# Keys and queries turned ahead of the values in a recurrent forward loop, and DMA issues moved between two queues in its backward loop

## The chip, the cores and the metric

The kernel runs on one core of a Trainium2 chip. TensorE (PE) multiplies matrices, VectorE (DVE), ScalarE (ACT) and GpSimd (POOL) work on tiles, and SyncE (SP) only issues DMA transfers; ScalarE and GpSimd issue some too, each from its own sequencer and in the order of its own instructions. The metric is the device time of one execution in microseconds, the median of several runs.

## The reference, cut to what matters

The program is a layer with a segmented recurrence, and its gradient for x, the first memory and seven weights.

```
xn = layernorm(x)                               # 2048 tokens of 640
mem = mem0                                      # 8 rows of 640
for s in range(64):                             # segments of 32 tokens
    h = concat([mem, xs])                       # 40 rows
    q, k, v = h @ Wq, h @ Wk, h @ Wv            # 32 heads of 128
    p = softmax(where(mask, q @ k.T * scale, -1e9))
    o = (p @ v) @ Wo
    mem, out_s = o[:8], o[8:]                   # the 8 rows go to the next segment
out = x + concat(out_s) * silu(FFN(xn))         # FFN: w1, w3, w2 with silu
grads = vjp(out)(grad_out)
```

The eight memory rows make both passes a chain of 64 steps: forward from segment 0 to 63, backward from 63 to 0.

## The kernel before, in words

Each engine's instructions stand in the order in which the program writes them (`in_order`), so the written text is the schedule. Two loops of 64 steps are touched.

**Forward** (`recurrence`). `chain(t, gap)` writes the chain of step t: it projects the memory rows, with 24 token rows that ride along, onto keys, queries and values, turns keys and queries so that heads lie on partitions (`packed_sel`), scores the eight memory queries, normalises, multiplies by values and by `Wo`, and folds the result into the next step's input `hx`. Between its parts it calls `gap("W0")`, `gap("W1")` and so on to `gap("G6")`. `FILL` puts independent work into these gaps: up to three pieces a step, here called units, each of four heads and the token rows of three segments. A unit goes through `ld` (rows are loaded), `turn_q`, `scores`, `soft_max`, `soft_exp`, `norm`, `turn_p` and `pv`. Steps come in threes, with 3, 3 and 2 units. `WARM` is a table of dummy products of TensorE (line 940) at the end of a gap.

`stage()` gives one of two staging buffers of 128x1024: in a step the keys take one (`sk`), the queries the other (`sq`), the values the first again (`sv`). So ScalarE's first copy into `sv` must follow the store of the keys (`dump(sk, k.KS...)`, line 635, issued by SyncE). Three banks of PSUM, `bA`, `bB` and `bC`, serve the whole chain by turns; five others (tag "x") serve the units.

**Backward** (`phase4_Abwd`). Here too `chain(t, gap)` is the chain and `gap_of` the filling. A unit is loaded by `ld` (four transfers: memory rows `QVM`, token rows of queries and values, token rows of the gradient, and probabilities `PR`), into one of four buffers, and goes through `turn`, `dprob`, `dsoft` and `gmem`; `gmem_ld` runs `gmem` and loads the next unit into the buffer that this frees. The chain loads its own state for the step to come: `loads` (values, probabilities, queries; SyncE), `load_k` (keys, four transfers) and `load_xp` (one). After three products with `WvT`, `WkT` and `WqT` the chain folds the sum of two halves: ScalarE copies one half (`fup`, line 351), VectorE adds (`gfsz`, line 355), TensorE turns it (line 370), and the next step begins.

SyncE's and ScalarE's transfers report on the same small set of completion semaphores, given out in the order of the program; a transfer whose semaphore is still in use waits for the earlier one to land.

## Time and profile before

| | us |
|---|---|
| median of 3 runs | 4686.83 (4672.63 to 4691.8) |
| the profiled execution | 4689.95 |
| its span, first to last instruction | 4688.2 |
| forward loop, 62 steps from 398.0 to 1548.5 | 1150.5 |
| backward loop, 62 steps from 1820.0 to 2885.9 | 1065.9 |

| engine | busy us | share of the span |
|---|---|---|
| TensorE | 4342.0 | 93% |
| VectorE | 2235.9 | 48% |
| GpSimd | 2110.7 | 45% |
| ScalarE | 1604.0 | 34% |

The profile gives each instruction's engine, line, tiles, start and length, and the idle time of its engine just before with what seems to have ended it. A `q` behind an engine's name (ACTq, SPq) is its sequencer, which issues DMAs; while ScalarE's sequencer issues, ScalarE computes nothing new. The clock is the share of TensorE's full clock that was granted: 1.00 or, in some windows of 3.4 us, 0.5.

### The profile page before, as it was taken

How to read it: one execution, taken by the hardware profiler on the slowest of the kernel's cores; microseconds unless marked ns; L12 is line 12 of the kernel's file. 1: busy time of each engine (PE TensorE's matmuls, PEld its weight loads, DVE VectorE, ACT ScalarE, POOL GpSimd, SP SyncE). 2: the span in 40 equal slices, each digit the busy share in tenths (PEclk: the TensorE clock that was granted, in tenths of full speed). 3: DMA queues.
4: the chain of work that ended last, by engine and by line, in shares of the span. 5: the costliest groups of instructions: out<-in, count | busy, mean ns of one | idle time of the engine just before them, and what ended most of it. 6: DMA issues, size and time to landing. Idle time of an engine off the chain costs nothing.

```text
span 4688.2 us, 155303 instructions
## 1 busy us (share of the span) xinstructions
PE 4342.0 (93%) x62272; PEld 2843.6 (61%) x62272; DVE 2235.9 (48%) x7158; ACT 1604.0 (34%) x4487; POOL 2110.7 (45%) x3531
## 2 busy tenths in 40 slices
PE   8998989999999887999989998999999999999999
PEld 4544656566666545666666665676667666666675
DVE  8734666666666434555555553343224332311460
ACT  5532555555554423333333332232223322200000
POOL 6542555555555324455444444454335543311440
PEclk9998999999999998999999998999999999999999
DMA  7773666666665777787777775654445543579783
GB/s 265 240 253 110 182 182 182 180 180 185 181 178 170 172 175 217 205 227 202 222 207 205 200 214 143 148 162 132 111 115 158 144 128 106 173 214 216 157 181 100
DMA packets 976826, 834.49 MB, mean 178 GB/s; under 512 B 518890, under 2 KB 858286, under 8 KB 974144
## 3 DMA queue, kind: packets, MB, share of 16 engines
q1 hardware_dynamic: 667943, 509.49, 39.6%
q0 software_dynamic: 129952, 228.13, 16.6%
q10 hardware_dynamic: 178211, 86.95, 7.5%
q8 instruction: 492, 8.06, 0.8%
q14 instruction: 228, 1.87, 0.1%
HBM read 472.66 MB, written 310.33 MB: 167 GB/s over the span
## 4 chain that ended last, share of the span: by engine, by line
PE 45%; DMA 11%; issue 4%; DVE 2%; ACT 2%; SPq 1%; ACTq 1%; POOL 1%; POOLq 0%; DVEq 0%
PE wg L1692 11%; PE g L1673 9%; PE bank L339 5%; PE oa L1839 4%; PE wa L2227 2%; PE r6p L1623 2%; PE t6g L1655 2%; DMA DSR<-kTT 1%; PE pgxb L2160 1%; PE bank L320 1%; PE bank L1259 1%; DMA kTT<-VTD 1%; DMA kTT<-GOS 1%; PE bank L552 1%; PE t L1613 1%
## 5 line engine op out<-in xcount | busy, mean ns | idle before, releaser
L1692 PE MATMUL wg<-gr,hr 128*128 128x512 bf16 x2400 | 521.7, 379 | 0.0
L1673 PE MATMUL g<-land,ghacc 128*128 128x320 bf16 x3072 | 459.2, 300 | 0.8
L320 PEld LDWEIGHTS <-hx 128*32 128x32 bf16 x10240 | 285.6, 98 | 267.2 <-issue 37.2
L1692 PEld LDWEIGHTS <-hr 128*128 128x128 bf16 x2400 | 233.9, 98 | 278.9
L1673 PEld LDWEIGHTS <-ghacc 128*128 128x128 bf16 x3072 | 288.8, 98 | 103.6 <-ACT ghacc L92 2.2
L903 POOL DMA_DIRECT2D OR<-xv x163 | 99.1, 608 | 398.8 <-ACT xv L92 334.7
L90 DVE CAST wgo<-wg 128x512 bf16<-128x512 f32 x72 | 49.8, 692 | 471.2 <-PE wg L1692 471.2
L339 PEld LDWEIGHTS <-gkv 128*8 128x8 bf16 x8192 | 194.0, 89 | 89.5 <-issue 3.6
L90 DVE CAST stg<-bank 128x512 bf16<-128x512 f32 x256 | 177.0, 692 | 136.9 <-PE bank L320 125.8
L1349 POOL DMA_DIRECT2D VTD<-gvT x176 | 129.7, 741 | 248.4 <-ACT gvT L1348 233.0
L92 ACT COPY ghacc<-t6g 128x768 bf16<-128x768 bf16 (+1 forms) x176 | 137.2, 780 | 295.2 <-PE t6g L1655 282.2
L1638 POOL DMA_DIRECT2D GSP<-grs x48 | 25.6, 542 | 457.4 <-ACT grs L1630 456.8
L1679 DVE TENSOR_TENSOR ghacc<-ghacc,g 128x320 f32<-128x320 f32 x192 | 93.7, 488 | 209.7 <-PE g L1673 209.7
L92 ACT CAST wgo<-wg 128x512 bf16<-128x512 f32 x48 | 28.1, 586 | 479.8 <-PE wg L1692 406.9
L92 ACT CAST stg<-bank 128x512 bf16<-128x512 f32 x128 | 75.3, 589 | 338.4 <-PE bank L328 155.7
L830 ACT ACTIVATE xP<-xsp,xnm 120x120 bf16<-120x120 f32 (+1 forms) x540 | 186.0, 366 | 13.7 <-DVE xnm L812 11.7
L850 POOL TENSOR_TENSOR xP<-xP,xrz 120x480 bf16<-120x480 bf16 x163 | 163.6, 1022 | 49.3 <-DVE xrz L849 39.7
L320 PE MATMUL bank<-WoT,hx 128*32 128x512 bf16 x2560 | 162.8, 404 | 11.3 <-DVE hx L1308 10.8
L339 PE MATMUL bank<-Wo,oTm 128*32 128x320 bf16 x4032 | 163.8, 319 | 9.1 <-DVE oTm L90 8.7
L339 PE MATMUL bank<-WvT,gkv 128*8 128x320 bf16 x4096 | 170.0, 324 | 0.8 <-issue 0.8
L320 PE MATMUL bank<-Wv,hx 128*32 128x512 bf16 x2560 | 161.4, 381 | 1.4 <-DVE kTT L652 0.6
L351 ACT COPY fup<-bank 64x160 f32<-64x160 f32 (+1 forms) x190 | 57.4, 334 | 307.8 <-DMA DSR<-kTT 142.8
(396 smaller groups left out, 10895.7 us busy)
## 6 DMA issues: line engine op xcount, KB each, us to landing
QVS<-stg SPq DMA_DIRECT2D x128, 256.0 KB
kTT<-VTD SPq DMA_DIRECT2D x64, 320.0 KB
PR<-xP POOLq DMA_DIRECT2D x168, 120.0 KB, 3.3
VTD<-gvT POOLq DMA_DIRECT2D x168, 120.0 KB, 4.3
land<-DSR SPq DMA_DIRECT2D x168, 120.0 KB
land<-PR SPq DMA_DIRECT2D x168, 120.0 KB
OR<-xv POOLq DMA_DIRECT2D x163, 120.0 KB, 3.3
orr<-OR SPq DMA_DIRECT2D x14, 1280.0 KB
```

Source lines behind the costliest of these rows:

```text
L90: return nc.vector.tensor_copy(out, in_)
L92: return nc.scalar.copy(out, in_)
L320: k.nc.tensor.matmul(bank[32 * g:32 * g + 32, :], x[:, dc, :], W[:, dc, c0:c0 + 512], start=(dc == 0), stop=(dc == k.DC - 1), tile_positio ...
L339: k.nc.tensor.matmul(pm[a][p0:p0 + nq, 0:320], x[:, h, :], W[:, h, 320 * b:320 * b + 320], start=(first and i == 0), stop=(last and i == 1 ...
L830: nc.scalar.activation(Pb[0:n, j, 0:n], sp[0:n, j, :], ACT.Exp, bias=nmx[0:n, j:j + 1], scale=k.scale, accum_out=Z[0:n, j:j + 1])
L850: eng.tensor_tensor(Pb[0:n, :, 0:n], Pb[0:n, :, 0:n], bc_last(rz[0:n], n), ALU.mult)
L903: q.dma_start(k.OR[120 * tl:120 * tl + n, c0:c0 + 512], v[0:n])
L1349: nc.gpsimd.dma_start(k.VTD[tl][:, :, h0:h0 + 4, :], vTq[:])
L1623: nc.tensor.matmul(pr[:, j * P:(j + 1) * P], lh[0:n, j, :], rw[i][0:n, j * P:(j + 1) * P], start=True, stop=True)
L1673: nc.tensor.matmul(pg[:], ring[:, i, j, r0:r0 + P], Ws[qd][i][:, j, 320 * h:320 * h + 320], start=(i == 0 and j == 0), stop=(i == 2 and j ...
L1692: nc.tensor.matmul(pw[:], hr[:, tl, dc * P:(dc + 1) * P], grs[i][:, tl, :], start=(tl == 0), stop=(tl == NF - 1))
L1839: nc.tensor.matmul(ac[j][i][:], orr[:, w, jj * P:(jj + 1) * P], gow[:, w, 320 * i:320 * i + 320], start=(w == 0), stop=(w == NW - 1))
```

## The change

Forward: the selections of the keys and then of the queries stand ahead of both halves of the value projection, with gap W1 (a unit's products) between the two and gap V0 behind them. The queries' selection uses bank `bA`, the first value half `bB`, and the memory scores `bA`. One warm product more stands in gap G5, and `turn_p` of the second unit moves from G5, ahead of the fold's turn, to G6, behind it.

Backward: `load_k`, `load_xp` and one of the two stores of memory rows into `DSR` are issued by SyncE and no longer by ScalarE. In gap G4 the two token-row transfers of the next unit are issued by ScalarE.

```diff
-        WARM = dict(G2=1, G3=2, G5=1)
+        WARM = dict(G2=1, G3=2, G5=2)
...
-            sv = stage()
-            packed_half(k, bA, hx, Wv, 0)
-            k.copy(sv[:, 0:512], bA[:], eng='s')
             qmT = ch.tile([P, H, 8], BF16, name="qmT", tag="fup")
-            pkk, pkq = [bview(b, P, 8, 4, 8) for b in (bC, bB)]
-            for pk, sg, dst in ((pkk, sk, kT[:, :, 40 * s:40 * s + 8]), (pkq, sq, qmT[:])):
+            for sg, b_, dst in ((sk, bC, kT[:, :, 40 * s:40 * s + 8]), (sq, bA, qmT[:])):
+                pk = bview(b_, P, 8, 4, 8)
                 packed_sel(k, pk, sg, 0)
                 packed_sel(k, pk, sg, 1)
                 nc.vector.tensor_copy(dst.rearrange("p (g j) c -> p j g c", g=4), pk[:])
+                if sg is sk:
+                    gap("W1")
             dump(sq, k.QVS[t // 4, :, :, t % 4, 0])
-            gap("W1")
+            gap("V0")
+            sv = stage()
+            packed_half(k, bB, hx, Wv, 0)
+            k.copy(sv[:, 0:512], bB[:], eng='s')
             packed_half(k, bC, hx, Wv, 1)
-            gap("V0")
...
-            psT = bview(bB, P, 2, 8, 16)
+            psT = bview(bA, P, 2, 8, 16)
...
-            ps2 = bview(bB, P, 2, 40)
+            ps2 = bview(bA, P, 2, 40)
...
-                    nc.tensor.matmul((bC if g == "G5" else bA)[:], k.ident[:], Wq[:, 0, 0:512], start=True, stop=True)
+                    nc.tensor.matmul((bC if g == "G5" else bB)[:], k.ident[:], Wq[:, 0, 0:512], start=True, stop=True)
...
             elif g == "G5":
-                at(turn_p, t, 0)
                 at(turn_q, t + 1, 0)
                 at(turn_q, t + 1, 1)
-                at(turn_p, t, 1)
+                at(turn_p, t, 0)
...
             elif g == "G6":
+                at(turn_p, t, 1)
                 at(pv, t, 0)
...
         def load_k(t):
-                nc.scalar.dma_start(kr[64 * a:64 * a + 8].rearrange("r (g c) -> r g c", g=2),
+                nc.sync.dma_start(kr[64 * a:64 * a + 8].rearrange("r (g c) -> r g c", g=2),
...
-                        nc.scalar.dma_start(dst, src[:, 2048 * a:2048 * a + 2048])
+                        nc.sync.dma_start(dst, src[:, 2048 * a:2048 * a + 2048])
...
-            nc.scalar.dma_start(xp[:], k.GXP[t // 3, :, :, t % 3])
+            nc.sync.dma_start(xp[:], k.GXP[t // 3, :, :, t % 3])
...
-                        (nc.scalar, nc.gpsimd)[a].dma_start(k.DSR[tl][nx + 8 * s:nx + 8 * s + 8, 16 * a:16 * a + 16, d0:d0 + c1 - c0],
+                        (nc.sync, nc.gpsimd)[a].dma_start(k.DSR[tl][nx + 8 * s:nx + 8 * s + 8, 16 * a:16 * a + 16, d0:d0 + c1 - c0],
...
+            qx = eng or nc.sync
...
-            k.load_x(qv, 0, k.x_src(tl, "qv", c0, c0 + 512), nc.sync)
-            k.load_x(gor, 0, k.g_src(tl, c0, c0 + 512), nc.sync)
+            k.load_x(qv, 0, k.x_src(tl, "qv", c0, c0 + 512), qx)
+            k.load_x(gor, 0, k.g_src(tl, c0, c0 + 512), qx)
...
                 elif g == "G4":
                     at(dprob, t, 2)
-                    at(gmem_ld, t, 0)
+                    at(lambda a, b: gmem_ld(a, b, nc.scalar), t, 0)
```

How the rows move is seen on ScalarE in one forward step, from a key copy of the gap W1 to the copy `sTm` of the memory scores. Before (`stg` is the value buffer, `xoT` and `xv` belong to a unit):

```order
L92 CAST stg<-bank_4107 128x512
L92 COPY kTT<-kpt 128x12x32
L92 CAST xoT<-xot 128x4x4x24
L895 DMA OTX<-xoT 128x4x96
L92 CAST xv<-xpo 120x512
L92 CAST stg<-bank_4109 128x512
L673 CAST sTm<-bank_4108 128x256
```

With the change:

```order
L92 COPY kTT<-kpt 128x12x32
L92 CAST xoT<-xot 128x4x4x24
L896 DMA OTX<-xoT 128x4x96
L92 CAST xv<-xpo 120x512
L92 CAST stg<-bank_4108 128x512
L92 CAST stg<-bank_4109 128x512
L674 CAST sTm<-bank_4107 128x256
```

The first value copy moved behind the unit's copies and its DMA issue. On ScalarE in one backward step, from the copies of the query gradient to the next step's first copy, before:

```order
L1291 ACTIVATE gqT<-bank_4109 128x2x64
L1291 ACTIVATE gqT<-bank_4108 128x2x64
L1192 DMA krb<-KS 8x2x1024
L1197 DMA krb<-KS 32x2x1024
L1192 DMA krb<-KS 8x2x1024
L1197 DMA krb<-KS 32x2x1024
L1298 DMA DSR<-kTT 8x16x8
L1298 DMA DSR<-kTT 8x16x32
L1204 DMA xp<-GXP 128x8x64
L351 COPY fup<-bank_4107 64x320
L1394 ACTIVATE gks<-gkp 128x4x3x8 x4
L92 CAST gstg<-bank_4108 128x512
```

With the change:

```order
L1292 ACTIVATE gqT<-bank_4109 128x2x64
L1292 ACTIVATE gqT<-bank_4108 128x2x64
L351 COPY fup<-bank_4107 64x320
L1396 ACTIVATE gks<-gkp 128x4x3x8 x2
L265 DMA kTT<-QVS 96x2x512
L265 DMA kTT<-GX 96x512
L1396 ACTIVATE gks<-gkp 128x4x3x8 x2
L92 CAST gstg<-bank_4108 128x512
```

Seven issues left ScalarE ahead of `fup`, and two came behind it. On SyncE in the same place, between the state loads (`VTD`, `PM`, `QM`) and the next state's, with the change:

```order
L1187 DMA kTT<-QM 128x1x128 x2
L1193 DMA krb<-KS 8x2x1024
L1198 DMA krb<-KS 32x2x1024
L1193 DMA krb<-KS 8x2x1024
L1198 DMA krb<-KS 32x2x1024
L1299 DMA DSR<-kTT 8x16x8
L1299 DMA DSR<-kTT 8x16x32
L1205 DMA xp<-GXP 128x8x64
L1334 DMA kTT<-QVM 24x2x512
L1338 DMA kTT<-PR 120x512
L1334 DMA kTT<-QVM 24x2x512
L265 DMA kTT<-QVS 96x2x512
```

Before, the first unit's `QVM` stood right behind the `QM` rows, followed by its own two row transfers and `PR`; these two are now absent from SyncE, and seven rows stand ahead.

## The prediction, made before the result was known

> **What bounds the kernel now.** I read the table of stages first, then the waits of TensorE in the two recurrent loops, then single steps engine by engine. In the table the columns are the stretch, its length, busy time of each engine (instructions), the granted clock, the busy share of the DMA engines and GB/s.

> ```profile
> 398.00:1548.50 1150.50, 1048.49 (x20659) 689.93 (x20659) 741.03 (x2107) 591.83 (x1970) 642.71 (x993) 0.97 0.62 176
> ...
> 1820.00:2885.90 1065.90, 963.59 (x22619) 670.21 (x22619) 553.46 (x2814) 355.70 (x1219) 505.07 (x914) 0.97 0.72 202
> ```

> The first row is 62 steps of the forward loop (18.6 us each), the second 62 steps of the backward loop (17.2 us each). TensorE is busy for 91% and 90% of them, and no other engine for more than 64%. So a step is TensorE's own list of work plus short holes, and only the holes, and the clock that falls after them, can be won. Everything outside these two rows is untouched. The holes of the forward loop, from the waits of TensorE and of ScalarE (total us, times, longest us):

> ```profile
> PE bank L681 <- ACT sTm L673: 30.7, 49, 2.1
> ...
> PE xpp L863 <- POOL xP L850: 15.8, 49, 2.0
> ...
> ACT stg L92 <- DMA KS<-stg: 93.0, 18, 8.6
> ```

> The longest is L681: the memory scores wait for ScalarE's copy `sTm`. A step whose L681 wait is long shows why (start, length, engine, line; in brackets the idle time before and its releaser):

> ```profile
> 1097.84 1.25 PE L320 MATMUL bank<-Wv,hx 128*32 128x512 bf16 x20
> ...
> 1100.82 0.59 ACT L92 CAST stg<-bank 128x512 bf16<-128x512 f32 x1 [4.35 <-DVE xPT L864]
> ...
> 1103.16 0.59 ACT L92 CAST stg<-bank 128x512 bf16<-128x512 f32 x1
> ...
> 1103.64 0.39 ACT L673 CAST sTm<-bank 128x256 bf16<-128x256 f32 x1
> ...
> 1104.09 0.22 PE L681 MATMUL bank<-ident,sTm 128*128 128x40 bf16 x2 [1.21 <-ACT sTm L673]
> ```

> ```profile
> 1096.62 0.34 SPq L635 DMA_DIRECT2D KS<-stg  x1
> ```

> The first half of the values is ready at about 1099.1, yet ScalarE copies it at 1100.82. It is the third `stage()` of the step and there are two buffers, so it takes the buffer of the keys, whose store was issued at 1096.62: the copy waits for that landing, 3.9 us. Behind it on ScalarE stand a copy of keys, `xoT`, a DMA issue, `xv`, the second value copy, and only then `sTm`.

> ```profile
> 1093.30:1112.80 19.50, 17.66 (x338) 11.39 (x335) 11.40 (x36) 9.89 (x33) 11.99 (x20) 0.91 0.63 176
> 1112.80:1130.70 17.90, 16.57 (x338) 10.88 (x336) 11.97 (x35) 9.68 (x33) 8.62 (x14) 1.00 0.60 170
> ...
> 440.00:840.00 400.00, 364.25 (x7234) 239.90 (x7227) 257.72 (x733) 214.36 (x705) 225.06 (x348) 0.98 0.64 181
> 840.00:1242.00 402.00, 365.52 (x7231) 242.95 (x7229) 258.29 (x739) 217.25 (x724) 232.91 (x359) 0.97 0.65 182
> ```

> This step ran at clock 0.91, the next, without the long wait, at 1.00: besides the hole, 19.5 x 0.09 = 1.8 us.

> In the backward loop the first hole is the fold: TensorE waits at L370 for VectorE's sum, which waits for ScalarE's copy `fup`.

> ```profile
> PE bank L370 <- DVE gfsz L355: 45.9, 62, 3.4
> ...
> PE ggpt L1352 <- DMA kTT<-GOS: 9.0, 9, 1.6
> ...
> PE gvpt L1345 <- DMA kTT<-QVS: 3.4, 4, 1.4
> ```

> ```profile
> 2206.32 0.28 ACTq L1192 DMA_DIRECT2D vt<-KS  x1
> 2206.84 0.32 ACTq L1197 DMA_DIRECT2D vt<-KS  x1
> 2207.20 0.38 ACTq L1192 DMA_DIRECT2D vt<-KS  x1
> 2207.75 0.32 ACTq L1197 DMA_DIRECT2D vt<-KS  x1
> 2208.47 1.40 ACTq L1298 DMA_DIRECT2D DSR<-kTT  x2
> 2209.91 0.56 ACTq L1204 DMA_DIRECT2D xp<-GXP  x1
> 2210.51 0.42 ACT L351 COPY fup<-bank 64x320 f32<-64x320 f32 x1 [6.59 <-DMA vt<-KS]
> ...
> 2211.34 0.51 PE L370 MATMUL bank<-sel,gfsz 128*128 128x8 bf16 x6 [2.99 <-DVE gfsz L355]
> ```

> `fup` starts 40 ns after the last of seven DMA issues on ScalarE's own sequencer: the issues held it, not TensorE. In the two stretches from there:

> ```profile
> 2193.60:2211.90 18.30, 14.76 (x367) 10.42 (x363) 9.74 (x52) 5.32 (x19) 9.00 (x17) 1.00 0.87 215
> 2211.90:2229.40 17.50, 16.77 (x375) 11.27 (x371) 8.03 (x40) 6.01 (x20) 8.21 (x16) 0.90 0.61 173
> ```

> **The change, part by part: forward.** TensorE's list is the same but for one 512-wide product. (a) ScalarE's `kTT`, `xoT`, issue and `xv` come before the value copies. The first value copy can now start at the end of the queries plus 0.2 (half of the selections) + 0.86 (the unit products) + 0.2 + 1.2 (half of the values) + 0.23 until a copy starts (rows under d), 2.7 us later: at 1100.5 in the step shown, about when the store lands; only the second value copy then stands before `sTm`. What is left of L681 is its floor. In the step from 1112.8 that wait is 0.24 us, so 49 x 0.24 = 12 of the 30.7 remain at most: 0 to 19 us, I take **15**, because VectorE's six small copies into `vt` also move later and end only just before the reduction. (b) The clock that falls with it: 400 x 0.02 + 402 x 0.03 = 20 us were lost in the stretches where these steps lie; 0 to 20, I take **10**. (c) `turn_p` of the second unit goes behind the fold, so the L863 wait for GpSimd's product shrinks: about a third of 15.8, **4** (0 to 10). (d) The loss: the queries are turned without the value half that covered VectorE's copy of them.

> ```profile
> 1135.22 1.25 PE L320 MATMUL bank<-Wv,hx 128*32 128x512 bf16 x20
> 1136.41 0.56 PE L328 MATMUL bank<-sel,stg 128*128 128x32 bf16 x16
> 1136.82 0.33 PE L761 MATMUL kpt<-ident,kr 96*128 96x96 bf16 x4
> ...
> 1137.68 1.26 PE L320 MATMUL bank<-Wv,hx 128*32 128x512 bf16 x20
> ```

> ```profile
> 1135.45 0.69 DVE L90 CAST stg<-bank 128x512 bf16<-128x512 f32 x1 [0.39 <-PE bank L320]
> ```

> The copy ends 0.92 us after the queries. The cover is now 0.2 of selections and the products between, 0.86 us here: enough. In every third step only one unit's product stands there (0.5 us, no kpt and no turn), which leaves 0.3 us; late in the loop the products are shorter still. About 20 x 0.3, and 3 for the rest: **+9** (0 to 18). (e) The extra warm product stands ahead of the fold, in the place of the L863 wait (15.8 / 49 = 0.3 us each); without that cover, at most 0.38 us (its row below) a step, 24 us in all. Banks only change names. Forward: -15 - 10 - 4 + 9 = **-20 us**.

> ```profile
> 1123.60 0.38 PE L940 MATMUL bank<-Wq,ident 128*128 128x512 bf16 x1
> ```

> **Backward.** (f) Seven issues leave ScalarE (3.3 us in the rows above, 0.28 to 0.70 each), two come to it, behind `fup` and the first `gks`. In an undisturbed stretch of three steps with the fold of a fourth, L370 waits

> ```profile
> PE bank L370 <- DVE gfsz L355: 1.5, 4, 0.6
> ```

> 0.38 us each, the fold's own latency: 62 x 0.38 = 23 of the 45.9 stay. 0 to 23, I take **19**. (g) The clock behind such holes: 17.5 x 0.10 = 1.8 us after the one shown; the loop at 0.97 loses about 32 us in all, and holes of this kind are some 0.6 of its avoidable waits: 0 to 20, I take **9**. (h) SyncE issues five more a step. Its idle time before the row loads of the fold gap:

> ```profile
> SPq L1332 <- PE gkp L1391: 209.5, 62, 6.3
> SPq L1332 <- DMA kTT<-VTD: 76.6, 39, 4.9
> ```

> is over 286 us, 4.6 us a step, against 3.3 us for the seven; and issued there, right behind the state loads, they start before ScalarE's would. Cost nothing; without that cover up to 3.3 us a step. (i) The two row transfers on ScalarE (0.59 and 0.54 us as issued now) lie before its next needed copy:

> ```profile
> L92 ACT CAST gstg<-bank 128x512 bf16<-128x512 f32 x62 | 36.3, 586 | 150.3 <-issue 139.2 <-PE bank L320 11.1
> ```

> 2.4 us idle each, which hides 1.1. SyncE reaches the next unit's rows 1.1 us sooner, so the row waits (9.0 + 3.4) shrink a little: **2** (0 to 12). Backward: -19 - 9 - 2 = **-30 us**.

> Sum: -50 on the profiled execution's 4689.95, which is 3 above the median of the runs: 4640, as a median **4637 us**.

> [...]

> **The rivals.** *SyncE becomes the queue that is late* (slower). Mechanism: the seven issues wait in order behind the state loads, and the row loads behind them; where the state loads end late, as in

> ```profile
> 2203.26 3.45 SPq L1186 DMA_DIRECT2D kTT<-QM  x2
> ...
> 2208.69 0.33 SPq L1332 DMA_DIRECT2D kTT<-QVM  x1
> ```

> only 2.0 us are free, the rows come some 2 us late and the clock falls (1.8): 3.8 us a step. It decides from about 13 such steps (50 / 3.8); in 25 of 62, with (a) to (d) and the fold still won: 4687 - 20 - 28 + 95 = 4734. Against it: the mean spare of 4.6. 8%. *The clock falls anyway*, whatever makes it fall is not these holes, and only the waits go: 4637 + 19 = 4656, 10%. *Forward gives nothing*: value copies right before `sTm` are as late as before, and (d) is paid: 4687 - 30 + 5 = 4662, 7%. *Backward gives nothing*: at a DMA share of 0.87 the rows turn up no sooner than they can be moved, and the fold's time returns as L1345 and L1352: 4667, 7%. *Nothing moves*, what is won in one third of the steps is lost in another: 4687, 6%.

> **How the numbers follow.** Forecast 62%, its own range 4600 to 4665 (the bounds of a to i, not all at once). The whole range: 4598, most of the bounds at their better end, to 4690, which takes in all rivals but the slower one; that and the forecast's far tail are what is left out. Half a per cent, about what a measurement of this kernel tells from no change, is 23 us: below 4663 lie most of the forecast (0.59), the clock rival (0.07) and half of the two one-sided ones (0.065), 0.73; slower is the SyncE rival, 0.08; 0.19 is between.

> **What would show it.** Forward: L681 from 30.7 to about 14 us; ScalarE's two value copies adjacent; no clock of 0.91 in every third step; a new wait of TensorE at the selections (L328) on VectorE's `stg`, under 12 us in total. Backward: L370 from 45.9 to under 28; no DMA issue between `gqT` and `fup`; SyncE's idle before the row loads down from 4.6 to 1 to 2 us a step. I am wrong if `sTm` still starts over a microsecond after its scores, if L1345 and L1352 together exceed 25 us, or if `gstg` on ScalarE waits for its own DMA issues.

## The result, and the profile after

The changed kernel takes 4652.74 us (median; 4647.98 to 4654.23), the kernel before 4684.54 us beside it on the same chip: a ratio of 0.9933, 95% interval 0.991 to 0.9955. The forecast was 4637 us within 4598 to 4690. Direction and range hold; the gain is about 32 us, not 50. The change was timed a second time among the experiments (0.9907, 0.988 to 0.9933); the two together give 0.992, some 36 us.

The table of stages of the changed kernel shows the two loops, 62 steps each (columns as in the prediction):

```profile
402.10:1552.10 1150.00, 1058.62 (x20717) 693.50 (x20718) 782.92 (x2106) 603.42 (x1970) 637.16 (x993) 0.98 0.62 176
1819.60:2851.90 1032.30, 952.11 (x22619) 665.71 (x22619) 553.06 (x2814) 355.88 (x1219) 504.46 (x914) 0.98 0.74 208
```

The backward loop went from 1065.9 to 1032.3 us. The forward loop of this execution stands where it stood: 1150.5 before, 1150.0 now. In it VectorE is busy for 783 us instead of 741, and TensorE for 1059 instead of 1048 us. The waits of TensorE, of the kernel before (rows not shown so far) and of the changed one (us in total, times, longest):

```profile
PE bank L681 <- ACT sTm L673: 32.2, 52, 2.1
PE bank L311 <- DVE Pm L692: 26.3, 37, 2.9
PE xpp L863 <- POOL xP L850: 19.3, 51, 2.7
...
PE bank L339 <- DVE oTm L90: 8.7, 41, 0.4
```

```profile
PE bank L311 <- DVE Pm L693: 58.1, 64, 3.5
PE bank L370 <- DVE gfsz L355: 26.1, 63, 0.6
PE bank L339 <- DVE oTm L90: 15.5, 55, 0.5
...
PE bank L682 <- ACT sTm L674: 8.7, 30, 0.5
...
PE ggpt L1354 <- DMA kTT<-GOS: 6.1, 7, 1.4
...
PE xpp L864 <- POOL xP L851: 3.7, 6, 2.7
```

(The lines have moved by one or two: L681 is now L682, L692 is L693, L863 is L864.) The wait on `sTm` fell by 23.5 us, more than forecast, and so did the one on GpSimd's product, by 15.6. But the next wait of the same chain, L311 on the normalised probabilities `Pm`, rose by 31.8, and L339 by 6.8. TensorE's extra warm product adds 10 us of busy time. What was won at two places was spent at three.

A step in which the keys' store lands late shows the new chain, in the timelines of VectorE, GpSimd, ScalarE and TensorE:

```profile
876.88 3.10 DVE L663 COPY vt<-stg 8x512 bf16<-8x512 bf16 x6 [1.88 <-ACT stg L92]
880.00 0.24 DVE L684 TENSOR_REDUCE mmx<-bank 128x2 f32<-128x80 f32 x1
```

```profile
877.40 1.25 POOL L663 COPY vt<-stg 8x512 bf16<-8x512 bf16 x2 [0.95 <-ACT stg L92]
878.71 0.28 POOL L619 COPY hx<-ride 128x120 bf16<-128x120 bf16 x1
878.94 0.89 POOL L875 COPY oTm<-oride 128x768 bf16<-128x768 bf16 x1
```

```profile
876.26 1.07 ACT L92 CAST stg<-bank 128x512 bf16<-128x512 f32 x2 [0.64 <-DMA KS<-stg]
877.63 0.37 ACT L674 CAST sTm<-bank 128x256 bf16<-128x256 f32 x1 [0.29 <-PE bank L672]
```

```profile
878.05 0.22 PE L682 MATMUL bank<-ident,sTm 128*128 128x40 bf16 x2
...
881.63 0.39 PE L311 MATMUL bank<-ident,Pm 128*128 128x128 bf16 x2 [2.18 <-DVE Pm L693]
```

`sTm` now starts as soon as its scores are done, and TensorE turns it at 878.05 without a wait. The reduction that begins the softmax, L684, could start at 878.3 us, when that turn ends. It starts at 880.0 us, because the six small copies of the values into `vt` stand ahead of it on VectorE and could not begin before ScalarE's value copies. They also take longer than before. The groups of VectorE in the forward loop, before and after:

```profile
L662 DVE COPY vt<-stg 8x512 bf16<-8x512 bf16 x372 | 111.3, 299 | 68.5 <-ACT stg L92 64.7
```

```profile
L663 DVE COPY vt<-stg 8x512 bf16<-8x512 bf16 x372 | 154.1, 414 | 94.1 <-ACT stg L92 89.9
```

The mean went from 299 to 414 ns: 43 us of VectorE's time, on the chain.

### The profile page after: what moved, and what is told of

Same layout as the page of the kernel before. It is cut to its first block, busy times and chain, and to the rows that moved or that the text cites. A ratio compares the mean times of both kernels' runs of the same rounds, so it can differ in the third digit from the quotient of the medians.

```text
span 4651.3 us, 155619 instructions
## 1 busy us (share of the span) xinstructions
PE 4338.8 (93%) x62336; PEld 2841.2 (61%) x62336; DVE 2277.9 (49%) x7158; ACT 1616.0 (35%) x4487; POOL 2103.7 (45%) x3531
## 4 chain that ended last, share of the span: by engine, by line
PE 62%; DMA 7%; DVE 5%; issue 5%; ACT 4%; SPq 1%; POOL 1%; ACTq 0%; POOLq 0%; DVEq 0%
PE bank L339 12%; PE wg L1694 11%; PE g L1675 9%; PE bank L320 7%; PE oa L1841 4%; PE wa L2229 2%; PE r6p L1625 2%; PE t6g L1657 2%; PE w2a L2085 1%; PE bank L1260 1%; PE pgxb L2162 1%; DMA kTT<-GOS 1%; DMA ggtok<-ggT 1%; PE bank L672 1%; PE bank L1288 1%
## 5 line engine op out<-in xcount | busy, mean ns | idle before, releaser
L320 PEld LDWEIGHTS <-hx 128*32 128x32 bf16 x10240 | 277.9, 97 | 254.1 <-issue 28.9
L90 DVE CAST wgo<-wg 128x512 bf16<-128x512 f32 x72 | 49.8, 692 | 471.2 <-PE wg L1694 471.2
L339 PEld LDWEIGHTS <-gkv 128*8 128x8 bf16 x8192 | 193.9, 89 | 89.8 <-issue 2.4
L92 ACT COPY ghacc<-t6g 128x768 bf16<-128x768 bf16 (+1 forms) x176 | 137.2, 780 | 292.6 <-PE t6g L1657 284.6
L90 DVE CAST stg<-bank 128x512 bf16<-128x512 f32 x256 | 177.0, 692 | 125.2 <-PE bank L320 111.1
L1640 POOL DMA_DIRECT2D GSP<-grs x48 | 25.6, 544 | 452.6 <-ACT grs L1632 452.6
L663 DVE COPY vt<-stg 8x512 bf16<-8x512 bf16 x384 | 158.9, 414 | 97.3 <-ACT stg L92 92.9
L851 POOL TENSOR_TENSOR xP<-xP,xrz 120x480 bf16<-120x480 bf16 x163 | 161.4, 993 | 87.7 <-DVE xrz L850 77.9
L92 ACT CAST wgo<-wg 128x512 bf16<-128x512 f32 x48 | 28.1, 586 | 479.8 <-PE wg L1694 392.5
L339 PE MATMUL bank<-Wo,oTm 128*32 128x320 bf16 x4032 | 169.8, 327 | 15.8 <-DVE oTm L90 15.5
L339 PE MATMUL bank<-WvT,gkv 128*8 128x320 bf16 x4096 | 170.3, 325 | 0.0
L320 PE MATMUL bank<-WoT,hx 128*32 128x512 bf16 x2560 | 153.5, 386 | 11.3 <-DVE hx L1309 10.9
L1398 POOL DMA_DIRECT2D GXP<-gks x157 | 92.2, 587 | 154.4 <-ACT gks L1396 149.9
L351 ACT COPY fup<-bank 64x160 f32<-64x160 f32 (+1 forms) x190 | 57.3, 334 | 300.7 <-PE bank L339 300.4
```

Source lines behind the costliest of these rows:

```text
L90: return nc.vector.tensor_copy(out, in_)
L92: return nc.scalar.copy(out, in_)
L320: k.nc.tensor.matmul(bank[32 * g:32 * g + 32, :], x[:, dc, :], W[:, dc, c0:c0 + 512], start=(dc == 0), stop=(dc == k.DC - 1), tile_positio ...
L339: k.nc.tensor.matmul(pm[a][p0:p0 + nq, 0:320], x[:, h, :], W[:, h, 320 * b:320 * b + 320], start=(first and i == 0), stop=(last and i == 1 ...
L663: (nc.gpsimd if b == 1 and g % 2 else nc.vector).tensor_copy(vt[p0:p0 + 8, c0:c0 + 512], sv[32 * g:32 * g + 8, b * 512:(b + 1) * 512])
L851: eng.tensor_tensor(Pb[0:n, :, 0:n], Pb[0:n, :, 0:n], bc_last(rz[0:n], n), ALU.mult)
```

## The experiments

"Clock lost" below is half the length of the stretches with granted clock 0.50 within a loop. Ratios are to the kernel before on the same chip, with their 95% intervals; as recorded they differ by up to 0.0015 from the quotient of the two medians. "Warm products" are the dummy products of the `WARM` table, which the expectations call unit products.

**1. Which part gains.** Four kernels on one chip. The forward part alone, on the backward loop of before:

> Only the forward part of the change. Theory (the forward wait was moved, not removed: ScalarE's copy sTm is on time, but VectorE's six copies into vt now end just before the reduction of the memory scores): about no change, 4676 to 4690 us, with L682 near 7 us and L311 near 50 us. Rival (the forward loop does gain its predicted 20 us and the even loop time of the one profile is chance): 4660 to 4668.

4658.2 us of 4682.5, 0.9958 (0.9939 to 0.9976). The waits are near those expected (L682 8.4 us, L311 53.2), but the expectation of no change in time fell. Yet its profile, though taken in the fastest of its ten executions (4646.6 us), does not show a faster forward loop of that size: 1136.9 us, 14 less, of which 10 are clock (29.0 us lost before, 18.8 here). Its backward loop, whose code is that of before, ran in 1038.3 instead of 1065.9:

```profile
399.30:1536.20 1136.90, 1050.56 (x20716) 690.51 (x20717) 780.35 (x2105) 603.11 (x1970) 634.68 (x991) 0.98 0.63 178
1803.40:2841.70 1038.30, 948.96 (x22619) 666.02 (x22619) 553.37 (x2814) 354.33 (x1219) 503.71 (x913) 0.98 0.73 207
```

So one and the same loop differs by 28 us between executions, and single profiles may not be compared by such sums alone.

The backward part alone:

> Only the backward part of the change. Theory: it holds the whole gain, 4648 to 4656 us, L370 near 26 us. Rival: half of the gain, 4665 to 4672.

4650.8 us, 0.9939 (0.9921 to 0.9956), as the theory had it. Its waits:

```profile
PE bank L681 <- ACT sTm L673: 35.6, 51, 1.9
PE bank L311 <- DVE Pm L692: 27.7, 39, 2.9
PE bank L370 <- DVE gfsz L355: 26.1, 63, 0.6
```

The forward waits are those of before, the backward one that of the change. The changed kernel with the two row transfers back on SyncE:

```diff
-                    at(lambda a, b: gmem_ld(a, b, nc.scalar), t, 0)
+                    at(gmem_ld, t, 0)
```

> The changed kernel with the two row transfers of gap G4 back on SyncE; the seven issues stay on SyncE. Theory (fup was held by ScalarE's own issues, and nothing else in the backward part matters): L370 stays near 26 us and the time within 6 us of the changed kernel, 4648 to 4660. Rival (SyncE has no room for seven more without giving two away, or the rows gain from ScalarE's queue): row waits L1347 and L1354 rise from 17 us to 30 or more, 4668 to 4685.

4644.0 us, 0.993 (0.9905 to 0.9955), a little under the expected 4648 to 4660, and L370 26.0: the seven issues that left ScalarE do it alone. This kernel has the whole forward part too, and on this chip it lies only 0.0009 (4 us) under the backward part alone, well inside the noise. The changed kernel with the old gap G5 (one warm product, `turn_p` ahead of the fold):

```diff
-        WARM = dict(G2=1, G3=2, G5=2)
+        WARM = dict(G2=1, G3=2, G5=1)
...
+                at(turn_p, t, 0)
                 at(turn_q, t + 1, 0)
                 at(turn_q, t + 1, 1)
-                at(turn_p, t, 0)
+                at(turn_p, t, 1)
...
             elif g == "G6":
-                at(turn_p, t, 1)
```

> The changed kernel with gaps G5 and G6 and the warm product as before. Theory (turn_p behind the fold takes away TensorE's wait for GpSimd, but the extra warm product and the fold's own sum take its place): L864 back to about 15 us, time within 6 us of the changed kernel, 4647 to 4659. Rival (that move is worth its 15 us and the rest of the forward part costs as much): 4662 to 4670.

4653.2 us, 0.9943 (0.9918 to 0.9969); L864 waits 10.5 us (about 15 expected) instead of 3.7, TensorE is busy 1050 us in the loop instead of 1059, and the loop takes 1149.8. The wait was replaced by a product of about the same length.

**2. The change once more, and ScalarE's order alone.** The change again, on the chip of the three that follow:

> The changed kernel itself, once more, so that it shares a chip with the three kernels beside it. Theory: the two parts add up. The forward part alone measured 24 us, the backward part alone 32 us, so the two together should come to about 4684 - 50 = 4634 us (4625 to 4643), and the forward loop's even time in the change's first profile (1150.0 against 1150.5 us) was one execution with many half-clock windows. Rival: the parts do not add up, and the change measures about 4650 us again (4646 to 4657).

4638.5 us of 4676.0, 0.9907 (0.988 to 0.9933). The time lies in the theory's range; the gain, 37.5 us, lies between theory and rival: the parts measured alone sum to 1.03% (0.42 and 0.61), the change measures 0.67 and 0.93. The intervals overlap, so nothing shows that the parts disturb each other. Its forward loop took 1156.0 us with 34.1 lost, again no shorter than before's.

The prediction's mechanism for the forward loop was ScalarE's order. This kernel changes that alone, on the kernel before:

```diff
             packed_half(k, bA, hx, Wv, 0)
-            k.copy(sv[:, 0:512], bA[:], eng='s')
...
             gap("V0")
+            k.copy(sv[:, 0:512], bA[:], eng='s')
```

> The kernel before, with one edit: ScalarE's copy of the first value half is written behind the second gap, next to the copy of the second half; TensorE's order is the old one. Theory (the prediction's mechanism for the forward part): what made sTm late was ScalarE's order, so L681's wait on sTm falls from 31 to about 14 us without any reordering of TensorE, while L311's wait on Pm rises from 20 towards 40 us, because VectorE's first four vt copies come later; the time is 0 to 15 us under before. Rival: the products' order matters (the copy of the queries waits for its products too), and L681's wait stays at 25 us or more.

4766.1 us of 4676.0, 1.0192 (1.0172 to 1.0212): 90 us slower. Its waits:

```profile
PE bank L311 <- DVE Pm L692: 116.5, 63, 2.9
...
PE bank L681 <- ACT sTm L673: 13.3, 44, 0.5
```

The theory on `sTm` holds to the microsecond: 13.3 of an expected 14, with TensorE's order untouched. What it says of time fell. The two value copies are adjacent, so none of the six `vt` copies can run before them, and L311 rose by 90 us (20 were expected). The first value half's early copy had been in `sTm`'s way but early for `vt`. (A third staging buffer, with which no value copy would wait for the keys' store, was not tried.) The table of stages adds a clock of 0.93 (87.0 us lost, before 29.0):

```profile
396.30:1638.80 1242.50, 1090.45 (x20658) 708.90 (x20659) 804.60 (x2106) 590.95 (x1970) 643.45 (x993) 0.93 0.57 163
```

**3. The `vt` copies out of the chain.** Two of VectorE's six (of the second half) written behind the normalisation, in the changed kernel (`vt_cp` is the same copy, put into a function; its place in the loop ahead is left out here):

```diff
...
             nc.vector.tensor_tensor(Pm, Pm, bc_last(rZm[:], 40), ALU.mult)
+            for g in (0, 2):
+                vt_cp(1, g, (0, 2))
             nc.gpsimd.dma_start(k.PM[t].rearrange("p (a c) -> p a c", a=2), Pm)
```

> The changed kernel, with VectorE's two second-half value copies (vt) written behind the chain's normalisation; GpSimd's two stay where they are. Theory: in the changed kernel the six vt copies of VectorE stand right ahead of the reduction that begins the chain to the scores' turn, and that is where the wait on sTm went: L311's wait on Pm, 50.1 us, falls to about 32 (62 steps x 0.3 us), and the kernel gains 10 to 20 us on the changed one. Rival: the wait is set by the staging buffer's late store or by the collision with GpSimd's copies; then L311's wait stays at 45 to 52 and the time within 5 us of the changed kernel's.

4656.0 us, 0.9961 (0.9946 to 0.9977), 18 us above the change, where the theory had 10 to 20 below it. L311 fell from 58 to 23, lower than the expected 32, but the wait reappears one link later:

```profile
PE bank L339 <- DVE oTm L90: 61.1, 60, 1.5
...
PE bank L311 <- DVE Pm L697: 23.3, 30, 2.9
```

VectorE's `oTm` copy is late instead. All four copies of the second half there, none on GpSimd:

> The changed kernel, with all four second-half value copies on VectorE behind the chain's normalisation and none on GpSimd, so that no GpSimd copy runs beside VectorE's. Theory (order and collision both cost): the mean of VectorE's vt copies falls from 0.41 to about 0.29 us, L311's wait on Pm from 50.1 to 20 to 30 us, and the kernel gains 15 to 25 us on the changed one. Rival: four copies behind the normalisation make VectorE's later work of the step (the turns' copies, the values' product) late, which appears as a longer wait of TensorE there; no gain, or a loss of up to 10 us.

4754.2 us, 1.0159 (1.0136 to 1.0182): far worse than the rival's 10 us, though L311 fell to 22.9 us as the theory had it. A step, VectorE and then TensorE:

```profile
1100.12 1.84 DVE L662 COPY vt<-stg 8x512 bf16<-8x512 bf16 x4
1101.99 0.66 DVE L815 TENSOR_REDUCE xmx<-xsp 120x4 f32<-120x480 f32 x1
...
1102.96 0.66 DVE L815 TENSOR_REDUCE xmx<-xsp 120x4 f32<-120x480 f32 x1
...
1103.73 0.41 DVE L90 CAST oTm<-bank 128x128 bf16<-128x128 f32 x1
```

```profile
1104.31 4.46 PE L339 MATMUL bank<-Wo,oTm 128*32 128x320 bf16 x64 [1.65 <-DVE oTm L90]
```

The copies push a unit's two reductions and `oTm` back. VectorE's work from the scores to the output projection is one chain: a copy put off is paid at its next link. But L339's wait, 87.7 us in all, is only 27 more than in the kernel above it, while the forward loop is 91 us longer (1258.2 against 1167.4). Most of that is clock: 102.4 us lost against 29.0, 73 more. This is where the clock became the question. The granted clock of this kernel over two steps, cut at the edges of the half-clock stretches (columns as above):

```profile
611.51:614.92 3.41, 3.26 (x52) 2.29 (x56) 0.87 (x5) 1.94 (x12) 2.02 (x3) 0.50 0.65 204
614.92:618.33 3.41, 3.36 (x67) 2.27 (x63) 1.47 (x5) 1.98 (x5) 1.56 (x3) 1.00 0.41 114
...
628.57:631.99 3.42, 1.76 (x32) 1.25 (x36) 3.16 (x11) 1.63 (x9) 0.70 (x1) 1.00 0.51 124
631.99:635.40 3.41, 3.41 (x53) 2.27 (x57) 1.82 (x6) 2.22 (x12) 2.22 (x3) 0.50 0.71 227
...
649.05:652.47 3.42, 1.89 (x29) 1.20 (x28) 3.12 (x11) 1.81 (x8) 2.03 (x3) 1.00 0.77 229
652.47:655.88 3.41, 3.16 (x49) 2.20 (x53) 2.10 (x7) 2.50 (x13) 1.93 (x3) 0.50 0.51 156
```

**4. The collision on `vt`, taken away.** In the changed kernel's trace, pairing records in time, the 186 `vt` copies of VectorE that run beside a GpSimd `vt` copy take 0.535 us on average, the 151 that run beside nothing 0.283, and the 30 beside a DMA issue of GpSimd (`OR`) 0.291. So GpSimd's copies, not its issues, seem to slow VectorE's. The average hides two cases. Of all 191 that share even a moment with a GpSimd `vt` copy, the 63 that began first took 0.28 to 0.29 us, and the 128 that began while GpSimd's ran took 0.60 to 0.73 and ended 0.14 to 0.15 us after it, every one. In the kernel before these were 64 and 19: the change made more of them begin second. This kernel takes its two `vt` copies from GpSimd: one to VectorE in the old place, one to ScalarE behind `sTm`.

```diff
...
-                    (nc.gpsimd if b == 1 and g % 2 else nc.vector).tensor_copy(
+                    (nc.scalar.copy if b == 1 and g == 3 else nc.vector.tensor_copy)(
```

> The changed kernel, with GpSimd's two second-half value copies (vt) taken off GpSimd: one goes to VectorE, in the old place, and one to ScalarE behind the copy sTm. Theory (collision): in the changed kernel's trace the 186 vt copies of VectorE that run beside a GpSimd vt copy take 0.535 us on average, the 151 that run beside none 0.283, and the difference, 47 us or 0.75 us a step, is the wait at L311. Without the GpSimd copies VectorE's mean falls from 0.41 to under 0.30 us although it does seven instead of six, L311's wait falls from 54 to 59 us towards 20 to 30, and the kernel gains 20 to 45 us on the changed one. Rival (order): seven copies ahead of the reduction are more work on the same chain, and the exponential waits for ScalarE's extra copy; L311's wait stays at 45 or more and the time within 8 us of the changed kernel's.

4672.4 us of 4677.7, 0.9982 (0.9959 to 1.0005): slower than the change, by more than the rival's 8 us too, and the theory's gain fell.

```profile
L662 DVE COPY vt<-stg 8x512 bf16<-8x512 bf16 x434 | 156.1, 360 | 90.4 <-ACT stg L92 85.4
```

Seven copies take 7 x 0.360 = 2.5 us a step, as the six did at 0.414. Those beside no GpSimd copy take 0.283 to 0.289; but GpSimd, done with `vt`, starts its next copy sooner (`oTm` from `oride`, 128x768, 0.84 us), and the 45 of VectorE's that meet this one take 0.995 on average. L311's wait stayed at 58.4 us, as the rival had it, and 51.2 us of clock were lost. The collision itself stands; taking one pair away only brought up the next. So what the collision alone costs, apart from the order of the copies, no run here shows.

**5. The clock by itself.** If holes cost clock by their place in a window, warm products put into a hole must win time though the late engine is as late as before. On the kernel with four late copies, five products in the gap before the output projection:

```diff
-        WARM = dict(G2=1, G3=2, G5=2)
+        WARM = dict(G2=1, G3=2, G4=5, G5=2)
...
-                    nc.tensor.matmul((bC if g == "G5" else bB)[:], k.ident[:], Wq[:, 0, 0:512], start=True, stop=True)
+                    nc.tensor.matmul((bC if g == "G5" else bA if g == "G4" else bB)[:], k.ident[:], Wq[:, 0, 0:512], start=True, stop=True)
```

> The kernel with all four second-half value copies on VectorE behind the normalisation (4754 us, 102 us of clock lost in its forward loop), with five unit products more in the gap ahead of the output projection, where its hole of 1.4 us a step lies. Theory (half-clock windows make the loss, and the hole's place in a fixed grid repeats because the step has come to six windows, 20.48 us): the products fill about 1.07 of 1.4 us, the clock lost falls from 102 to under 40 us and the time to 4670 to 4700, though VectorE is as late as before. Rival: the loss comes from the late copies themselves, and the time stays above 4735.

4677.4 us of 4677.7, 0.9994 (0.9973 to 1.0016), where without them it was 1.0159. The forward loops, without and with:

```profile
395.30:1653.50 1258.20, 1126.90 (x20717) 726.86 (x20717) 800.23 (x2230) 602.52 (x1970) 562.22 (x869) 0.92 0.56 161
```

```profile
396.20:1570.10 1173.90, 1106.74 (x21027) 706.92 (x21028) 800.39 (x2230) 602.15 (x1970) 561.91 (x867) 0.99 0.61 172
```

VectorE is busy for the same 800 us; the loop is 84 us shorter, the clock lost 6.8 instead of 102.4. That these losses are clock and not the copies' own cost is shown. The same on the changed kernel, two products more ahead of the probabilities' turn:

```diff
-        WARM = dict(G2=1, G3=2, G5=2)
+        WARM = dict(G2=3, G3=2, G5=2)
```

> The changed kernel, with three unit products in place of one in the gap ahead of the probabilities' turn (two more, of 0.2 us each, in the hole of 0.9 us that L311 waits in). They compute nothing that is used. Theory (the clock is judged in fixed windows of 3.41 us: over eight traces no half-clock window followed a window with under 0.5 us of TensorE idle time, about 40 in 100 one with 1.2, nearly all one with 2): the products shorten the hole without shortening the wait, so L311's listed wait falls by about 20 us, and the clock lost in the forward loop falls from 27 to 34 us to under 18; the kernel gains 8 to 20 us. Rival: such products do not count for the clock, or the steps whose hole is short pay for them; no gain, or up to 20 us slower.

4634.4 us of 4677.7, 0.9893 (0.986 to 0.9927); L311's listed wait 26.2, clock lost 13.7, the loop 1135.5:

```profile
402.40:1537.90 1135.50, 1072.13 (x20841) 696.05 (x20842) 782.90 (x2106) 603.42 (x1970) 636.64 (x991) 0.99 0.63 178
```

One product more before the output projection (`G4=1`), and the row loads on SyncE:

> The kernel with three unit products ahead of the probabilities' turn (4634 us), with one unit product more in the gap ahead of the output projection, where L339 waits 16 us in 62 steps (0.26 us each), and the backward loop's two row loads back on SyncE. Theory: L339's wait falls under 6 us, the forward loop's lost clock stays under 18 us, the row loads make no difference; 4618 to 4634 us, a ratio to the kernel before of 0.987 to 0.990. Rival: the product stands in the way of a projection that did not wait in many steps (0.2 us each), and the time rises to 4636 to 4650.

4633.4 us of 4668.3, 0.9917 (0.99 to 0.9935). The ratio misses the expected 0.987 to 0.990. In the forward loop all of it came: L339 waits 2.2 us, 5.1 of clock are lost, and its 1126.5 us are the shortest of all runs:

```profile
401.00:1527.50 1126.50, 1078.84 (x20902) 694.87 (x20903) 780.06 (x2105) 603.51 (x1970) 635.89 (x991) 1.00 0.62 180
1791.30:2836.80 1045.50, 956.89 (x22619) 667.57 (x22619) 553.13 (x2814) 355.55 (x1219) 504.82 (x914) 0.97 0.74 205
```

The backward loop of this execution took 1045.5 with 27.3 lost, 13 to 20 longer than the change's, and the ratio lies between the change's own two (0.9933 and 0.9907). Both fillings make the forward loop shorter in the profile; that either beats the change in time is not shown.

## Why the prediction was right or wrong, point by point

**Backward (-30; measured about -29).** (f) -19: L370 went from 46.5 to 26.1, -20, and the seven issues alone do it. (g) -9: with the old backward code three executions lost 35.8, 20.5 and 30.7 us of clock (29 on average), with the new one eleven lost 13.7 to 29.0 (21 on average): about -8, smaller than the spread between executions. The loops themselves: 1065.9, 1038.3 and 1052.5 (mean 1052) against eleven from 1024.6 to 1045.5 (mean 1033), -20 us; by time the part alone measured -29 (-21 to -37). (h) 0: right. The longest of SyncE's waits before the row loads shows what the issues used up, from 209.5 us to

```profile
SPq L1334 <- PE gkp L1393: 90.0, 87, 3.3
```

and the rows of the rival "SyncE becomes the late queue" did not come: TensorE's waits for transfers at the two row lines are 17.0 us after, 16.0 before, and 15.6 when the change was run again. Nor did the other two signs of being wrong: `sTm` starts 0.08 us after its scores in 63 of 64 steps, and `gstg` never within 1.6 us of ScalarE's last issue ahead of it. (i) -2: not there, and the row transfers on ScalarE were worth nothing that can be told from the run without them. The trace of (f) now reads as forecast, with no issue between `gqT` and `fup`:

```profile
2179.36 0.48 ACT L1292 ACTIVATE gqT<-bank 128x128 bf16<-128x128 f32 x2
2183.60 0.42 ACT L351 COPY fup<-bank 64x320 f32<-64x320 f32 x1 [3.76 <-PE bank L339]
```

**Forward (-20; measured about -4 to -20).** (a) The mechanism was right for the wait on `sTm`, and isolated by the kernel that moves one copy. Its size was -23 instead of -15. The step that failed is the sentence beside it: that `vt`'s copies "end only just before the reduction" was priced within 15 us. They end after it could start, by 1.7 us in the step shown, because they begin later and because 128 of them, not 19, begin while GpSimd's copy runs and take 0.65 us on average instead of 0.28. L311 gained 31.8 us. The prediction had no term for that line. That the `vt` copies make this wait is shown (two of them moved: 58 to 23 us); how much of it is their later start and how much the collision is not. (b) -10: the new forward loop lost 27.3, 34.1, 18.8, 22.2 and 27.3 us in five executions, 26 on average, before 29.0 and 25.6: nothing to speak of. The hole had moved, not gone, and windows with a hole of one to two microseconds were often followed by half clock (111 of 421 with 0.9 to 1.3 us idle, 143 of 254 with 1.3 to 1.7). The sign named for it, no clock of 0.91 in every third step, did not come either: 13 of 62 steps ran below 0.95, before 15. (c) -4, measured -15.6, and (e) 0, a product of 0.2 us in 62 steps, belong together: of the 15.6, some 7 are the product standing in the place of the wait (10.5 to 3.7), which wins nothing; where the other 9 come from no run isolates. (d) +9: the new wait at the selections is small, 1.7 us in 8 steps at L328.

So in waits the forward part is a draw, and the loop says so: 1150.0, 1156.0, 1136.9 and 1143.5 us with it, 1150.5 and 1151.6 without. By time, the part alone measured -20 (-11 to -29); the change less the backward part gives -8, and the kernel with the row loads on SyncE less the backward part -4, each with 12 us or more either way. Whether it is 4 or 20 us is open. If it is 20, it agrees with the forecast by luck: the waits that were to give it came out even.

**The rivals.** "Forward gives nothing" had the right place (value copies ahead of the chain) and the wrong engine: it let ScalarE's `sTm` be late, where it was VectorE's reduction. "The clock falls anyway" is half true: in the forward loop it fell as before (26 us lost on average, before 29.0 and 25.6).

**What came ahead of half clock.** The half-clock stretches at 631.99 and 652.47 us follow windows in which TensorE was busy for 1.76 and 1.89 us of 3.41: here a window that was idle in part was enough.

## What to carry to other kernels

Taking away one wait of a serial chain moves the hole to the next link, so follow the chain to its end: here from ScalarE's `sTm` to VectorE's small copies, to `Pm`, to `oTm`. Price what stands ahead of each link on its engine, and what the engine next to it does at that moment (VectorE's copies took 0.65 us instead of 0.28 where they began during one of GpSimd). Where a hole of a microsecond cannot be closed, try products in it that nobody uses: with four late copies the wait before the output projection came to 87.7 us and the clock lost to 102.4, and five products a step there left 6.8 of the latter.

## What the runs showed of the hardware

**Half clock followed windows in which TensorE was idle in part.** Over fourteen traces, from 410 to 2850 us, I cut the time at the grid and compared TensorE's idle time in a full-clock window with the clock of the next. Under 0.5 us idle: 4 of 7132 were followed by half clock. 0.5 to 0.9: 37 of 1297 (3%). 0.9 to 1.3: 111 of 421 (26%). 1.3 to 1.7: 143 of 254 (56%). Over 1.7: 200 of 213 (94%). A hole that lies across the edge of two windows is split between them in this count. That single profiles of the same loop differ by 20 to 30 us may come from a grid that lies differently over the steps in each run; no run isolates it. The loop with four late copies, whose step with its loss came to 20.48 us, six windows, from 611 to 1000 us, repeated the loss there step after step (the loop's loss 102 us against 29).

**A copy of VectorE that began during a copy of GpSimd ended after it.** In the changed kernel the same 8x512 bf16 copy on VectorE took 0.283 us alone and 0.29 beside a DMA issue of GpSimd. Beside GpSimd's copy of the same size (0.61 us) it took 0.28 to 0.29 when it began first, and 0.60 to 0.73 when GpSimd's began first; then it ended 0.14 to 0.15 us after GpSimd's, in all 128 cases. In the kernel with seven `vt` copies on VectorE and one on ScalarE, those that met a GpSimd copy of 128x768 (0.84 us) took 0.995 on average. GpSimd's copy was not longer where only a VectorE copy that had begun first met it: 0.604 us on average in the kernel before (64 times), and 0.612 where the two did not meet (45).
